# A weight's load moved behind the turn of u, and two x chunks loaded between the z writes, in a Fourier-filter and FFN kernel

## The chip, the cores and the metric

The kernel runs on one core of a Trainium2 chip. The metric is the device time in microseconds (us) of one execution. Every run of a kernel is paired with runs of the kernel before on the same chip.

## The reference

```python
X = np.fft.rfft(x, axis=1)                    # x: 8 batches, 3008 rows, 256 columns
Y = X * (filt_r + 1j * filt_i)[None, :, :]
y = np.fft.irfft(Y, n=3008, axis=1)           # 24064 rows in all
h = np.maximum(y.reshape(24064, 256) @ w_in, 0.0)   # w_in 256 x 2048
out = (h * h) @ w_out                               # w_out 2048 x 256, float32
```

The kernel does the transform in matmul stages (a: x to u, b: u to products with the filter, P: products to z, y: z to y). u and z go through DRAM to be turned. The FFN is a row of numbered steps: each computes two blocks of h for a group of 512 rows (psH), and half of an output tile of the group before (psO). The transforms of batches 1 to 7 are spread over those steps by a plan; batch 0's transform is the prologue, ahead of the first FFN step.

## The kernel before

These are the parts that the change touches, cut. Tiles of one pool and one tag take turns in the same bytes: `p_h2` has two buffers for the tag `h2`.

```python
def load_win():
    w32s[0] = p_h2.tile([128, 2, DFF], F32, tag="h2", name="win32")     # fp32 copy
    nc.sync.dma_start(out=w32s[0], in_=moe_w_in.rearrange(...))
def cast_win():                                # four GpSimd casts to fp16
    for k in range(4):
        nc.gpsimd.tensor_copy(out=sWin[...], in_=w32s[0][...])
def cast_wout(k):                              # one of four VectorE casts
    nc.vector.tensor_copy(out=sWout[...], in_=w32s[1][...])
...
uT = p_h2.tile([128, 2, NC, 128], F16, tag="h2", name="uT")   # batch 0's u, to be turned
...                                            # casts of x, constants
load_win()
cast_win()
for c in (0, 2, 1, 3):
    chunk_a0(c)                                # matmuls of stage a, copies to uT
for k in range(6):
    turn_u(k)
...                                            # 14 rounds of stages b and P:
    if r == 7:
        load_x(1, 0); cast_x(1, 0, nc.gpsimd)  # first x chunk of batch 1
    if r == 10:
        read_z(0, 0, (0,))
...
chunk_a(1, 0)                                  # stage a of that chunk
load_wout()
load_x(1, 1); load_x(1, 2)
... read_z(0, c) ...
write_u(1, 0)
keep_warm(14)                                  # unused matmuls on zeros
for n in range(4):
    unit_y(0, n)                               # first y; then the FFN steps start
```

## Time and profile before

| kernel before | |
|---|---|
| median of its runs beside the changed kernel | 848.89 us (848.24 to 850.38, 4 runs) |
| profiled run | 849.39 us, span 847.3 us, mean granted clock 0.977 |
| TensorE busy | 787.1 us, 93% |

The page cuts the span into 40 slices of 21.2 us. The digit is the busy share of TensorE (PE), or its granted clock, in tenths.

```profile
span 847.3 us, 14755 instructions
...
PE   3297888789999999999999999999999999999998
...
PEclk7599999999999999999999999999999999999999
```

The time is in the 9s, and they are full; only the first ten digits leave room. The prediction reads that room. Timeline columns: start, duration, engine, line, operation, and in brackets the idle time before it and what ended it.

```profile
73.70 1.02 PE L346 MATMUL psA<-x,sC 94*96 94x512 f16 x4 [2.09 <-POOL x L313]
...
75.28 4.81 PE L250 MATMUL warm<-zero 128*128 128x512 f16 x14 [0.56 <-DVE u L356]
...
79.93 0.27 PE L483 MATMUL psY<-zero 128*128 128x256 f16 x1
...
87.70 0.69 DVE L305 CAST sWout<-wout 128x1024 f16<-128x1024 f32 x1 [0.34 <-DMA wout<-in_moe_w_out_dram]
...
94.71 0.38 PE L327 MATMUL psA<-x,sC 94*96 94x512 f16 x1 [1.52 <-DVE x L313]
```

They are stage a of batch 1's first x chunk ahead of the FFN, the unused matmuls that are meant to keep the clock up (`keep_warm`), the first y, the first cast of W_out, and the first stage-a matmul inside the FFN steps.

### The profile page before, as it was taken

The page shows a single profiled execution, that of the slowest core. Times are in us where ns is not written, and L with a number is a line of the kernel's source. Part 1 is how long each engine was busy: PE and PEld are TensorE (multiplying, and loading weights), DVE is VectorE, ACT ScalarE, POOL GpSimd, SP SyncE. Part 2 cuts the span into 40 slices and gives each one's busy share as a digit, 9 for nine tenths or more (in the row PEclk, how much of TensorE's full clock was granted, in tenths as well). Part 3 has the DMA queues.
Part 4 walks back from the last instruction along what each step waited for, and adds up shares of the span by engine and source line. Part 5 has one row for each costly group of instructions (what it writes and reads, how often), then busy time and mean ns, then how long its engine had stood idle before and what let it go on. Part 6 is the DMA issues. An engine that isn't in the chain of part 4 may idle for free.

```text
span 847.3 us, 14755 instructions
## 1 busy us (share of the span) xinstructions
PE 787.1 (93%) x6084; PEld 554.0 (65%) x6084; DVE 548.7 (65%) x876; ACT 553.6 (65%) x709; POOL 30.8 (4%) x44
## 2 busy tenths in 40 slices
PE   3297888789999999999999999999999999999998
PEld 1273555566677766676677766686676767676666
DVE  3174856655896569955896569955896569753332
ACT  0174755567677767777677767777776767766663
POOL 4200013200000000000000000000000000000000
PEclk7599999999999999999999999999999999999999
DMA  9308844443467255633556255633466252341111
GB/s 365 160 13 235 203 135 137 125 113 100 142 163 169 65 160 138 180 82 100 160 146 171 62 161 137 181 82 100 148 155 168 62 164 63 90 98 38 38 38 51
DMA packets 87930, 107.94 MB, mean 127 GB/s; under 512 B 6208, under 2 KB 78656, under 8 KB 83392
## 3 DMA queue, kind: packets, MB, share of 16 engines
q1 hardware_dynamic: 87512, 106.59, 44.7%
q8 instruction: 47, 0.77, 0.4%
q10 hardware_dynamic: 288, 0.43, 0.2%
q14 instruction: 19, 0.16, 0.1%
q0 software_dynamic: 64, 0.00, 0.0%
HBM read 58.76 MB, written 48.23 MB: 126 GB/s over the span
## 4 chain that ended last, share of the span: by engine, by line
PE 79%; DMA 11%; DVE 5%; POOL 2%; ACT 1%; issue 1%; SPq 1%; POOLq 0%; DVEq 0%; ACTq 0%
PE psO L530 35%; PE psH L515 33%; PE psA L327 3%; DMA ut<-dU 3%; PE psY L485 2%; PE psB L408 2%; DVE prod L411 2%; PE psP L444 2%; DMA win<-in_moe_w_in_dram 2%; DMA f<-in_filt_r_dram 2%; DMA x<-in_x_dram 2%; DMA zt<-dZ 1%; DMA dZ<-ze 1%; DVE h L523 1%; POOL yf L420 1%; POOL yf L419 1%
## 5 line engine op out<-in xcount | busy, mean ns | idle before, releaser
L519 ACT ACTIVATE h<-psH 128x1024 f16<-128x1024 f32 x376 | 385.1, 1025 | 196.9 <-PE psH L515 196.9
L530 PE MATMUL psO<-sWout,h 128*128 128x256 f16 x3008 | 389.4, 273 | 2.6 <-DVE h L523 2.6
L515 PE MATMUL psH<-yt,sWin 128*128 128x512 f16 (+7 forms) x1728 | 387.9, 352 | 2.6 <-DVE yt L494 1.9
L530 PEld LDWEIGHTS <-h 128*128 128x128 f16 x3008 | 290.8, 98 | 82.4 <-DVE h L523 2.8
L523 DVE TENSOR_TENSOR h<-h 128x1024 f16<-128x1024 f16 x376 | 254.1, 685 | 100.8 <-ACT h L519 99.5
L515 PEld LDWEIGHTS <-sWin 128*128 128x128 f16 x1728 | 159.7, 98 | 103.3 <-issue 4.9
L411 DVE TENSOR_TENSOR prod<-psB,sF 128x1024 f16<-128x1024 f32 x96 | 116.7, 1220 | 11.4 <-PE psB L408 8.2
L494 DVE CAST yt<-psY 128x376 f16<-128x376 f32 x64 | 35.1, 549 | 64.5 <-PE psY L485 64.5
L446 ACT CAST ze<-psP 128x512 f16<-128x512 f32 x96 | 56.0, 586 | 31.1 <-PE psP L444 27.6
L334 DVE CAST u<-psA 96x512 f16<-96x512 f32 x54 | 37.1, 686 | 48.4 <-PE psA L327 48.4
L537 ACT COPY ost<-psO 128x512 f32<-128x512 f32 x94 | 55.4, 589 | 7.5 <-PE psO L530 5.8
L426 DVE TENSOR_TENSOR yf<-prod,yf 128x512 f16<-128x512 f16 x84 | 35.7, 425 | 19.4 <-POOL yf L420 17.0
L485 PEld LDWEIGHTS <-zt 112*128 112x128 f16 x512 | 34.8, 98 | 15.1 <-issue 5.1
L485 PE MATMUL psY<-sC,zt 112*128 112x94 f16 x512 | 42.1, 205 | 2.5 <-DMA zt<-dZ 2.5
L327 PE MATMUL psA<-x,sC 94*96 94x512 f16 x108 | 41.2, 381 | 1.5 <-DVE x L313 1.5
L408 PE MATMUL psB<-ut,sSB 128*128 128x256 f16 x192 | 36.6, 272 | 5.1 <-DMA ut<-dU 2.6
L444 PE MATMUL psP<-yf,sSP 128*128 128x256 f16 x168 | 32.4, 275 | 6.5 <-DVE prod L411 4.4
L408 PEld LDWEIGHTS <-sSB 128*128 128x128 f16 x192 | 18.7, 98 | 26.8 <-issue 7.5
L492 ACT CAST yt<-psY 128x376 f16<-128x376 f32 x64 | 29.8, 467 | 6.3 <-PE psY L485 6.2
L313 DVE CAST x<-x 94x2048 f16<-94x2048 f32 x27 | 32.8, 1217 | 0.0
L369 PE MATMUL psA<-sC,x 128*128 128x96 f16 x64 | 8.8, 246 | 25.5 <-ACT uT L377 25.3
L332 ACT CAST u<-psA 96x512 f16<-96x512 f32 x54 | 30.9, 572 | 0.9 <-DMA x<-in_x_dram 0.9
(53 smaller groups left out, 239.8 us busy)
## 6 DMA issues: line engine op xcount, KB each, us to landing
x<-in_x_dram SPq DMA_DIRECT2D x24, 768.0 KB
dZ<-ze SPq DMA_DIRECT2D x32, 384.0 KB
zt<-dZ SPq DMA_DIRECT2D x64, 192.0 KB
dU<-u SPq DMA_DIRECT2D x28, 384.0 KB
out_dram<-ost SPq DMA_DIRECT2D x32, 256.0 KB
out_dram<-ost SPq DMA_DIRECT2D x64, 128.0 KB
ut<-dU SPq DMA_DIRECT2D x7, 1024.0 KB
ut<-dU SPq DMA_DIRECT2D x7, 512.0 KB
```

The costliest lines, as they stand in the source:

```text
L327: nc.tensor.matmul(ps[0:96, :], sSA, x16s[(b, c)][:, 2 * i:2 * i + 2, :], start=True, stop=True)
L334: nc.vector.tensor_copy(out=o, in_=pv)
L408: nc.tensor.matmul(ps[:, i * D:(i + 1) * D], sSB[:, 2 * p + i, :], uts[b][:, 2 * p + i, :], start=True, stop=True)
L411: nc.vector.tensor_mul(out=prod, in0=ps.rearrange("p (a d) -> p a d", d=D).unsqueeze(1).to_broadcast([128, 2, 2, D]), in1=sF[:, :, 2 * p:2 ...
L444: nc.tensor.matmul(ps[:, i * D:(i + 1) * D], sSP[:, c2, :], prod[:, i, :], start=True, stop=True)
L446: nc.scalar.copy(out=zes[(b, c)][:, 2 * i6:2 * i6 + 2, :], in_=ps.rearrange("p (a d) -> p a d", d=D))
L485: nc.tensor.matmul(ps[:, 94 * jj:94 * jj + 94], zt[:, 4 * (g % 2) + jj, dt * 128:(dt + 1) * 128], sSY, start=True, stop=True)
L515: nc.tensor.matmul(ps[:, i, o:o + n], sWin[:, dt, jt * 128:(jt + 1) * 128], yts[b][:, dt, r:r + n], start=(dt == 0), stop=(dt == 1))
L519: nc.scalar.activation(out=h2[:, 2 * s:2 * s + 2, :], in_=ps, func=AF.Relu)
L523: nc.vector.tensor_mul(out=v, in0=v, in1=v)
L530: nc.tensor.matmul(pso[g][:, t % 2, :], h2s[g][:, jt, t * 128:(t + 1) * 128], sWout[:, jt, :], start=(jt == 0), stop=(jt == NJT - 1))
L537: nc.scalar.copy(out=ost, in_=pso[g])
```

## The change

uT takes the bytes that hold the fp32 copy of W_in until that is cast. The intent of the first part is to turn the order round: u is turned first, and W_in takes over the buffer. The second part loads two chunks of batch 1's x in the prologue instead of one, and moves batch 1's plan ahead by up to two steps.

```diff
-    load_win()
-    cast_win()
-
     for c in (0, 2, 1, 3):
         chunk_a0(c)
...
         turn_u(k)
+    load_win()
+    cast_win()
...
-        if r == 7:
-            load_x(1, 0)
-            cast_x(1, 0, nc.gpsimd)
+        if r in (5, 8):
+            load_x(1, r // 8)
+            cast_x(1, r // 8, nc.gpsimd)
...
-    chunk_a(1, 0)
+    for c in range(2):
+        chunk_a(1, c)
     load_wout()
-    load_x(1, 1)
     load_x(1, 2)
+    load_x(1, 3)
...
-    write_u(1, 0)
-    keep_warm(14)
+    for c in range(2):
+        write_u(1, c)
+    keep_warm(10)
... and in the plan of batch 1:
-            for c in range(1, 4):
-                put(5 + 2 * c, 0, cast_x, 1, c)
-            put(7, 0, load_x, 1, 3)
-        t0 = 6
-        for a in range(4 if b == 1 else 0, 16):
+            for c in range(2, 4):
+                put(3 + 2 * c, 0, cast_x, 1, c)
+        t0 = 4 if b == 1 else 6
+        for a in range(8 if b == 1 else 0, 16):
...
-        put(14, 1, read_u, b)
-        t0 = 17 if b == 1 else 18
+        put(12 if b == 1 else 14, 1, read_u, b)
+        t0 = 16 if b == 1 else 18
...
-            r = t0 + (16 if b == 1 else 19) * p // 11
+            r = t0 + (17 if b == 1 else 19) * p // 11
```

## The prediction

> **What bounds the kernel now.** I read the windows view first, cut where the kind of work changes, to see where TensorE (the PE column) is not full. Columns: window, length, busy time and count of each engine, granted clock, DMA share, GB/s.
>
> ```profile
> 0.00:34.00 34.00, 6.86 (x22) 2.65 (x23) 6.63 (x11) 1.28 (x1) 13.98 (x19) 0.65 0.82 327
> 34.00:80.00 46.00, 37.12 (x367) 29.17 (x367) 25.98 (x28) 24.62 (x36) 2.11 (x2) 0.89 0.29 78
> 80.00:95.00 15.00, 11.11 (x75) 5.50 (x74) 10.48 (x17) 10.31 (x13) 0.00 (x0) 1.00 1.05 266
> 95.00:115.00 20.00, 19.31 (x140) 12.62 (x138) 13.05 (x20) 13.38 (x19) 0.00 (x0) 1.00 0.63 180
> 115.00:165.00 50.00, 39.73 (x273) 26.45 (x274) 32.54 (x46) 26.76 (x35) 14.69 (x24) 0.97 0.45 128
> 300.00:830.00 530.00, 527.91 (x4047) 373.96 (x4045) 365.35 (x602) 375.93 (x474) 0.00 (x0) 1.00 0.43 116
> ```
>
> From 300 to 830 TensorE is busy 527.9 of 530: nothing there is touched by the change and nothing there can be won. What can be won is ahead of 180 us: 27 us of TensorE idle before 34, and 10 us between 115 and 165. So the second view is the timeline of the start, and the third that of VectorE (DVE) after 115.
>
> ```profile
> 10.42 0.26 PE L371 MATMUL psA<-sC,x 120*128 120x96 f16 x1 [2.69 <-DVE x L611]
> 12.18 2.02 POOL L611 CAST x<-x 128x1024 f16<-128x1024 f32 x2 [9.51 <-DMA x<-in_x_dram]
> 15.82 0.39 SPq L293 DMA_DIRECT2D win<-in_moe_w_in_dram  x1
> ...
> 30.22 4.00 POOL L301 CAST sWin<-win 128x1024 f16<-128x1024 f32 x4 [7.97 <-DMA win<-in_moe_w_in_dram]
> 30.25 1.28 ACT L377 ACT_TABLE_LOAD   x1 [30.25 <-DMA win<-in_moe_w_in_dram]
> 34.25 0.48 ACT L377 CAST uT<-psA 128x384 f16<-128x384 f32 x1 [2.72 <-POOL sWin L301]
> 34.78 0.24 PE L369 MATMUL psA<-sC,x 128*128 128x96 f16 x1 [23.63 <-ACT uT L377]
> ```
>
> TensorE starts batch 0's first transform at 10.42 and stops after a few matmuls for 23.6 us. It waits for ScalarE to copy the first result into uT. ScalarE waits for the last W_in cast. uT has the same bytes as the fp32 copy of W_in, so W_in must arrive (30.2) and be cast (34.2) before uT may be written. A weight that nobody reads before 81.8 us holds up everything.
>
> ```profile
> 115.06 0.39 PE L408 MATMUL psB<-ut,sSB 128*128 128x256 f16 x2 [0.49 <-DMA ut<-dU]
> ```
>
> ```profile
> 115.49 1.23 DVE L411 TENSOR_TENSOR prod<-psB,sF 128x1024 f16<-128x1024 f32 x1 [1.04 <-PE psB L408]
> 118.16 0.43 DVE L426 TENSOR_TENSOR yf<-prod,yf 128x512 f16<-128x512 f16 x1 [1.45 <-POOL yf L420]
> 118.50 0.69 DVE L523 TENSOR_TENSOR h<-h 128x1024 f16<-128x1024 f16 x1
> 119.11 1.22 DVE L411 TENSOR_TENSOR prod<-psB,sF 128x1024 f16<-128x1024 f32 x1
> 121.69 0.43 DVE L426 TENSOR_TENSOR yf<-prod,yf 128x512 f16<-128x512 f16 x1 [1.36 <-POOL yf L420]
> ```
>
> From 115 to 164 the second batch's twelve products run on VectorE, each followed by a 1.4 us wait for two GpSimd copies; the squares of the FFN queue behind. VectorE has no other idle time there: it sets the pace.
>
> **What the Trainium skill says.** "TensorE: Matmul & The Clock Gate", Part 1, says an idle TensorE falls to half clock and needs a free-running window of about 3.4 us of activity to come back. The trace agrees: after the long idle the 96-column matmuls start 0.08 us apart until 40.5, and 0.045 apart from 41.35. "SBUF — State Buffer", "SBUF: two separate sides", says that GpSimd and VectorE exclude each other on a shared port only where VectorE uses both its ports or has two SBUF inputs. The new GpSimd cast will lie beside products that read one operand from PSUM, so by that page it should not block; no run yet shows it. "DMA: Bandwidth & Descriptors", "Issuing engines are not separate DMA queues", says all DMAs share sixteen engines and interleave. The 80 to 95 window, with a DMA share of 1.05, agrees: W_out, issued at 76.35, was first used at 87.70, 11.3 us for 2 MB, while W_in alone moved at about 430 GB/s.
>
> **The change, part by part.**
>
> *1. W_in behind the turn of u.* uT's first write no longer waits for W_in. The list of waits of the built kernel shows what is left: the same bytes held the third x piece, so the first copy waits for its load (landed 12.18) and its two GpSimd casts (done 14.2). The ScalarE table load needs only the load and hides under the casts. The first copy thus moves from 34.25 to 14.2: 20.0 us. It does not gain the full 23.6 us of the idle. Work behind it must be ready 20 us earlier: the filter casts end at 22.3 and are first used at 49.06 - 20.0 = 29.0; the DFT constants had landed when W_in began to move, about 24.5, and are used at 34.8. Both fit. W_in itself is now issued when the turn's last matmul is done (48.2 - 20.0 = 28.2), needs about 5 us for its 2.1 MB plus about 2, and 4.0 for the casts: ready near 39.5, against a first use near 61.8. Hidden. The clock recovers at about the same distance from the start of work, give or take 1 us. So the whole prologue moves by 20.0.
>
> *2. Two x chunks between the z writes.* The second chunk takes, in time, the place of the one there was: issued behind the second z write, landing some 6 us later, cast in 1.9. In before the first matmul on it began at 73.70, 2.1 us after the last unit; now the first chunk's four matmuls (1.0 us) fit into that hole, and the second starts near 53.7. No cost, and no gain here either: y waits for the z write (72.26, 3.15 us) and the reads behind it, which move by 20.0 only. Four fewer warming matmuls save nothing if y waits for z; at best 1 us, which step 4 eats.
>
> *3. The FFN steps behind.* Four psA matmuls leave the steps. Before: from the first psA (94.71) to the first psB (115.06) 20.35 us: six steps with two psA each, 13.05 us or 2.175 each, two steps with y, then a step in which psB waits for ut. After: four steps at 2.175 (8.70), two bare ones at 1.74 (3.48; the distance of bare steps near 170 us), and the y steps with the following psH, 107.76 to 112.50 (4.74): 16.92 us. The first psB comes 3.43 us earlier. Its data is there: the last copy of u ended 13.1 us after the first psA and ut landed 7.2 later; now 8.7 + 7.2 = 15.9, 1 us in hand. The VectorE chain then has the same 12 products, GpSimd waits and sums, the same two x and two y casts, but by the listing of both builds 17 squares in place of 16: +0.60. Both kernels issue the last product in step 33, so what follows is alike. Net 2.8.
>
> *4. Contention, given back.* W_out and two x chunks share the engines as before, but the second x issues about 2 us earlier and one more u write of 0.4 MB follows (its wait list holds it until W_out has landed). VectorE waited only 0.3 us for W_out and was then packed until 94.6, so a late W_out or a late x counts in full. An estimate: 0.39 MB at the 266 GB/s of that window is 1.5 us, of which I take 0.6.
>
> Sum: 848.4 - 20.0 - 2.8 + 0.6 = 826.2 us; I predict 826.
>
> **Rivals.**
> *A, the wait changes its name.* Constants, filter casts or the x piece replace W_in, and the prologue gains only 15 or so. For it: the DMA engines are full from 3 to 29 us. Against it: the landing times above leave 5 us or more for each. It would give about 831.
> *B, W_out's loading becomes the floor.* FFN steps 3 to 7 need W_out, issued only behind the z reads. If x takes bandwidth from it, 2 to 3 us of the gain go. For it: DMA share 1.05 in 80 to 95 and VectorE packed behind it. Against it: W_out's issue moves by the same 20 us. It would give about 828.
> *C, the gain is swallowed later.* If VectorE's chain in the second batch were tied to something absolute, earlier arrival would become waiting. Against it: the trace shows it waiting only for GpSimd and its own order, all of which move. It would give 840 or more; I give it almost nothing.
> *D, more than the sum.* If the clock comes up a window sooner, or y starts earlier because warming ends sooner, 1 to 3 us more: 823 to 825.
>
> **Range and chances.** The 20.0 is read off two recorded times and is good to 1 us; the 2.8 rests on two chains and is good to 1.5; the contention may be 0 to 2.5. Together 822.5 to 829.5 should hold it 8 times in 10. Two per cent is 17 us, a limit of 831.4; even with all of step 3 lost and 2 us of contention the first step alone gives 830. Faster 0.95, same 0.04, slower 0.01.
>
> **What would show it right or wrong.** Step 1: ScalarE's first uT copy at 14.2 behind a GpSimd x cast, no idle of 20 us on TensorE, W_in cast near 35 to 40. Wrong if that copy starts later, or TensorE waits for a filter cast or a constant. Step 2: the second chunk's matmuls near 53.7, y near 60. Step 3: from first psA to first psB about 17 us, from the first product to the last sum of batch 1 about 49 us. Step 4: first W_out cast near 67.7 to 68.5; later means rival B. From 180 us on both traces must match, shifted; a stretch there with TensorE idle would prove me wrong.

## More of the kernel before

The three batches of experiments ran on three different chips, so kernels of different batches are compared only through their ratios to the kernel before.

## The result, and the profile after

The changed kernel takes 824.38 us (median of 4 runs: 826.93, 823.8, 822.26, 824.96), against 848.89 before. The ratio is 0.971, with a 95% interval from 0.9678 to 0.9742. A ratio is the mean time of one kernel's runs over that of the other's of the same rounds, so it is not quite the ratio of the medians. The outputs are correct.

The profile is of the 826.93 us run, the slowest of the four. The same three lines of its page:

```profile
span 824.8 us, 14748 instructions
...
PE   5878987999999999999999999999999999999998
...
PEclk7998999999999999999999999999999999999999
```

The 3 and the 2 at the start have become 5 and 8. The windows view of the changed kernel (length, then busy time and count of TensorE, weight loads, VectorE, ScalarE and GpSimd; granted clock, DMA share, GB/s) shows where it still has room:

```profile
0.00:34.00 34.00, 21.32 (x230) 16.39 (x231) 17.09 (x25) 9.86 (x15) 10.18 (x15) 0.85 0.81 313
34.00:60.00 26.00, 22.02 (x175) 15.88 (x174) 16.84 (x16) 17.33 (x25) 7.77 (x6) 0.93 0.68 187
60.00:75.00 15.00, 10.59 (x59) 4.68 (x57) 9.61 (x16) 9.33 (x13) 0.00 (x0) 0.92 1.05 267
75.00:92.00 17.00, 16.54 (x107) 10.55 (x107) 9.77 (x15) 9.89 (x14) 0.00 (x0) 0.87 0.47 125
92.00:142.00 50.00, 41.11 (x294) 27.00 (x292) 33.00 (x47) 29.00 (x38) 13.40 (x22) 0.99 0.43 125
...
280.00:806.00 526.00, 524.65 (x4027) 371.97 (x4025) 363.73 (x600) 373.16 (x470) 0.00 (x0) 1.00 0.42 116
```

In the first 34 us TensorE is busy 21.3 us instead of 6.9. The late part is as full as it was. What is new lies between 60 and 92: DMA share 1.05, TensorE idle for 4.4 us, then a granted clock of 0.87. The timeline of the changed kernel gives the events:

```profile
12.02 1.28 ACT L377 ACT_TABLE_LOAD   x1 [12.02 <-DMA x<-in_x_dram]
14.03 0.48 ACT L377 CAST uT<-psA 128x384 f16<-128x384 f32 x1 [0.73 <-POOL x L610]
...
28.31 0.39 SPq L293 DMA_DIRECT2D win<-in_moe_w_in_dram  x1
...
37.18 3.99 POOL L301 CAST sWin<-win 128x1024 f16<-128x1024 f32 x4 [15.15 <-DMA win<-in_moe_w_in_dram]
...
54.37 1.02 PE L346 MATMUL psA<-x,sC 94*96 94x512 f16 x4 [1.89 <-POOL x L313]
55.23 4.01 PE L250 MATMUL warm<-zero 128*128 128x512 f16 x10
...
56.11 0.42 SPq L297 DMA_DIRECT2D wout<-in_moe_w_out_dram  x1
...
59.08 0.27 PE L483 MATMUL psY<-zero 128*128 128x256 f16 x1
...
68.46 0.69 DVE L305 CAST sWout<-wout 128x1024 f16<-128x1024 f32 x1 [1.89 <-DMA wout<-in_moe_w_out_dram]
...
75.47 0.59 PE L327 MATMUL psA<-x,sC 94*96 94x512 f16 x1 [0.89 <-DVE x L313]
75.84 1.91 PE L530 MATMUL psO<-sWout,h 128*128 128x256 f16 x8
...
94.24 0.38 PE L408 MATMUL psB<-ut,sSB 128*128 128x256 f16 x2
```

ScalarE's first copy to uT has moved from 34.25 to 14.03, and it now waits for a GpSimd cast of x instead of the W_in casts. W_in is ready at 41.2, long before the first FFN step. The first y moves by 20.85 us. In both kernels it starts right behind the last unused matmul, with no idle time between (no bracket on its line): TensorE does not wait for z there. VectorE then waits 1.89 us for W_out (0.34 before), and some time behind that a group of eight psO matmuls takes 1.91 us where it usually takes 1.04: TensorE is at half clock. The windows view in stretches of 3.4 us, laid so that one starts where the half clock does, shows what came ahead of it:

```profile
65.50:68.90 3.40, 3.37 (x25) 1.77 (x24) 1.13 (x2) 3.40 (x5) 0.00 (x0) 1.00 1.05 236
68.90:72.30 3.40, 1.64 (x11) 0.65 (x9) 3.40 (x7) 2.22 (x4) 0.00 (x0) 1.00 1.00 214
72.30:75.70 3.40, 1.67 (x4) 0.55 (x4) 3.40 (x6) 1.24 (x2) 0.00 (x0) 0.52 1.01 216
75.70:79.10 3.40, 3.40 (x13) 1.88 (x12) 1.19 (x3) 0.58 (x1) 0.00 (x0) 0.50 0.63 190
```

VectorE has no idle time from 68.9 to 75.7 (3.40 of 3.40, twice): it works off what the late W_out held up. TensorE waits for it and is busy 1.64 of 3.40 us. In the next stretch its clock is halved, and stays so for a further one until it has been busy throughout. So the late weight goes with two costs in this profile: 1.9 us of wait, and half clock behind it.

The starts of the same events, from the timelines of six profiled runs (the last four are experiments below; "rest" is from the last sum of batch 1's filter products to the end of the span):

| start of, us | before | changed | warm_steps | warm_both | before_both | wout_pool |
|---|---|---|---|---|---|---|
| first copy of u | 34.25 | 14.03 | 14.21 | 14.15 | 34.25 | 11.24 |
| first y matmul | 79.93 | 59.08 | 59.40 | 59.02 | 78.54 | 58.88 |
| first W_out cast (VectorE) | 87.70 | 68.46 | 66.81 | 69.91 | 85.89 | - |
| first psA in the steps | 94.71 | 75.47 | 74.86 | 76.91 | 93.94 | 72.03 |
| first psB of batch 1 | 115.06 | 94.24 | 91.78 | 93.83 | 114.24 | 88.94 |
| last sum of batch 1 | 163.66 | 143.36 | 140.96 | 142.94 | 163.41 | 138.12 |
| rest | 683.6 | 681.4 | 678.8 | 681.0 | 679.8 | 681.8 |
| span | 847.3 | 824.8 | 819.8 | 823.9 | 843.2 | 819.9 |

Before against changed, stage by stage: to the first y -20.85, to the first W_out cast +1.61, to psA 0.00 (7.01 us in both), to psB -1.58, to the last sum +0.52, rest -2.2. Together -22.5 us of span, for this slowest run of the changed kernel.

### The profile page after: what moved, and what is told of

It reads as the page before. It is cut to its first block, busy times and chain, and to the rows that moved or that the text cites.

```text
span 824.8 us, 14748 instructions
## 1 busy us (share of the span) xinstructions
PE 787.3 (95%) x6080; PEld 553.7 (67%) x6080; DVE 547.7 (66%) x874; ACT 553.4 (67%) x708; POOL 32.6 (4%) x45
## 4 chain that ended last, share of the span: by engine, by line
PE 83%; DMA 8%; DVE 6%; POOL 2%; ACT 1%; issue 1%; SPq 0%; POOLq 0%; DVEq 0%; ACTq 0%
PE psO L530 36%; PE psH L515 34%; PE psA L327 3%; PE psY L485 2%; DMA ut<-dU 2%; PE psB L408 2%; DVE prod L411 2%; PE psP L444 2%; DMA wout<-in_moe_w_out_dram 1%; DVE h L523 1%; DMA x<-in_x_dram 1%; DMA dZ<-ze 1%; DMA zt<-dZ 1%; POOL yf L420 1%; POOL yf L419 1%
## 5 line engine op out<-in xcount | busy, mean ns | idle before, releaser
L426 DVE TENSOR_TENSOR yf<-prod,yf 128x512 f16<-128x512 f16 x84 | 35.7, 425 | 19.4 <-POOL yf L420 16.9
L419 DVE COPY yf<-prod 64x512 f16<-64x512 f16 x72 | 20.9, 290 | 2.5
```

## The experiments

Twelve kernels ran, four to a batch: a_again, p1_only, p2_only and own_early on one chip (median of the kernel before there: 849.45 us), warm_steps, x3_late, late_plan and wout_pool on a second (848.14), the last four on a third (848.22). All gave correct outputs, and all were timed in five rounds.

### The change again, and its two parts alone

The first is the changed kernel with no edit. The other two are the kernel before with one part of the diff above.

```diff
# p1_only: load_win() and cast_win() behind turn_u, nothing else
# p2_only: the two x chunks and the new plan; load_win() and cast_win() stay ahead of chunk_a0
```

> The changed kernel once more, unaltered, for a second profile and more times. In its first profile TensorE ran at half clock from 72.7 to 79.3 us, because it had idled while VectorE waited for W_out; I put the cost at 1.9 us (18.77 us instead of 16.92 from the first psA matmul to the first psB). If that drop depends on where the clock's window happens to fall, the second profile may lack it and then shows about 17 us there. If it belongs to the schedule, the profile shows 18.5 to 19 us again. Time: 822 to 827 us, median near 824.5.

> Only the first half of the change: W_in is loaded and cast behind the turn of u, everything else as before. My theory (shared bytes held the start back by 20.0 us, the rest of the schedule only moves): first uT copy near 14.1 us, total 848.9 - 20.0 = 829 us (828 to 830.5). Rival C (later stages swallow part of it): 833 or more. If this half alone gives 824 to 825, then the second half is worth nothing.

> Only the second half: two x chunks of batch 1 between the z writes and the shifted plan of batch 1, with W_in loaded early as before. My theory: the step from the first psA matmul to the first psB is about 17 us instead of 20.35, the chain on VectorE about 0.5 us longer, and W_out some 1 us later: 846 to 847 us. If it alone gives 843 to 844, the whole surplus over 20 us comes from it; if it is 848 to 849, the plan is worth nothing and the surplus comes from elsewhere.

Measured: a_again 826.78 us (822.92 to 827.75, 5 runs), ratio 0.9724 [0.9697, 0.975]. p1_only 829.31 (827.59 to 833.97, 6 runs), 0.9771 [0.9743, 0.9798]. p2_only 844.32 (842.1 to 847.97, 6 runs), 0.9946 [0.992, 0.9972].

By means, p1_only gains 19.7 us, p2_only 5.0, and both together 23.9: the parts add up within the intervals. The first is the 20.0 of the prediction. In p1_only's trace the first copy of u starts at 14.28. The first y, at 61.40, moves by only 18.5 us there: the cast of x ahead of it moved by 19.4, and TensorE was at half clock for the four matmuls on that chunk (1.86 us, 1.02 before). The second part gained more than the 2.2 us that I had left of it (2.8 less 0.6); its interval, 2.4 to 6.8 us, holds the 2.8 but not the 2.2. The 846 to 847 us expected of p2_only were missed. Its six times, too, have a gap (842.1 to 842.96, and 845.67 to 847.97), and its profile, of the slowest, shows what the changed kernel's does: 1.81 us of wait for W_out, then half clock and 19.09 us from psA to psB.

The changed kernel's nine times so far lie, by eye, in two groups, 822.3 to 825.0 and 826.8 to 827.8. a_again's profile, from the upper group, again shows a wait for W_out (2.23 us) and half clock from 73 to 80 (18.71 us from psA to psB). That raised the question of the next batches: what separates the groups?

### W_in early, but uT in other bytes

```diff
-    uT = p_h2.tile([128, 2, NC, 128], F16, tag="h2", name="uT")
+    uT = sF[:, 1].rearrange("p c d -> p (c d)").rearrange("p (t c q) -> p t c q", t=2, c=NC)
```

This is the kernel before in its order. Only the bytes of uT differ: a part of sF that is not yet in use.

> The kernel before with its order kept (W_in loaded and cast early), but uT put in bytes that nobody else uses at that time, those of the half of sF that is written after the turn. It separates the shared bytes from the early load itself. My theory, that only the sharing cost time: the first uT copy comes when the first matmuls are done, near 11.1 us, 23 us earlier than before, and the total is about 826 us (824.5 to 827.5), although W_in still arrives near 30 us. Rival (the early W_in load itself delays the start through the DMA engines): the first copy stays later than 14 us and the total is above 829 us.

Measured: 826.78 us (825.83 to 828.77, 4 runs), ratio 0.974 [0.9717, 0.9763]. ScalarE in its timeline:

```profile
1.61 1.28 ACT L377 ACT_TABLE_LOAD   x1 [1.61 <-PEq L700]
11.20 0.48 ACT L377 CAST sF<-psA 128x384 f16<-128x384 f32 x1 [8.30 <-PE psA L371]
```

The copy waits for its matmul and for nothing else, although W_in still goes first and is cast only from 31.38. So it was the shared bytes that held up u, not W_in's place in the queue. This gains 22.4 us by means without moving a load.

### Unused matmuls in FFN steps 3 to 7

```diff
             ffn_g1(g, k)
+            if g == 0 and k >= 3:
+                keep_warm(3)
```

This is the changed kernel with three matmuls on zeros in each of those steps, so that TensorE does not fall to half clock while VectorE works off W_out.

> The changed kernel with three dummy matmuls on zeros (0.2 us each) after the first product of each of the FFN steps 3 to 7, where TensorE otherwise idles for W_out's casts. Two profiles of the changed kernel had half clock there and its nine times fall in two groups, 822 to 825 and 826.8 to 827.8. My theory (whether the clock falls depends on where its window lies, and costs about 1.8 us): the profile shows the full clock from 62 to 92 us, about 17 us from the first psA to the first psB matmul instead of 18.7, and times of 821 to 825 us, with the upper group thinned. Rival (the spread comes from the DMA engines or from elsewhere): the times stay at 822 to 828 with a median above 825, or get longer.

Measured: 822.82 us (820.85 to 822.91, 5 runs), ratio 0.9691 [0.9668, 0.9714].

```profile
66.81 0.69 DVE L305 CAST sWout<-wout 128x1024 f16<-128x1024 f32 x1
...
74.86 0.38 PE L327 MATMUL psA<-x,sC 94*96 94x512 f16 x1 [0.60 <-DVE x L313]
...
91.78 0.38 PE L408 MATMUL psB<-ut,sSB 128*128 128x256 f16 x2
```

From psA to psB it is 16.92 us, the prediction's number, and the clock is full from 62 to 92. The missing 1.85 us of the changed kernel's 18.77 was half clock. But W_out also came without a wait in this profile, which no unused matmul explains. I took the absence of the upper group for the clock's doing; warm_both below shows that this was too quick.

### The last x chunk's load later

```diff
     load_x(1, 2)
-    load_x(1, 3)
... in the plan of batch 1:
+            put(3, 1, load_x, 1, 3)
```

> The changed kernel with the load of the fourth x chunk of batch 1 moved from the prologue to FFN step 3, behind W_out. It tests the term for contention. My theory (W_out was slowed by the second x load issued beside it): W_out reaches VectorE in about 11.3 us after its issue instead of 12.3 and 12.8, VectorE waits for it 1 us less, and the time falls by 0.5 to 1.5 us against the changed kernel. Rival (W_out is slow because of the z reads and the total bytes, not this load): W_out still takes over 12 us, same time.

Measured: 824.04 us (822.32 to 826.52, 5 runs), ratio 0.9711 [0.9687, 0.9735]: no gain on the changed kernel's 0.971 and 0.9724. The theory was that this load slows W_out. The timeline says no:

```profile
55.38 0.42 SPq L297 DMA_DIRECT2D wout<-in_moe_w_out_dram  x1
...
68.48 0.69 DVE L305 CAST sWout<-wout 128x1024 f16<-128x1024 f32 x1 [1.47 <-DMA wout<-in_moe_w_out_dram]
```

From the issue of W_out to its first cast it is 13.1 us with that load out of the way. With it in place, profiles show 12.35 (changed), 14.02 (a_again), 11.1 (late_plan) and at most 10.6 (warm_steps). So W_out can be late without this load. One profile among times that differ so much does not exclude that the load has some share. The added u write is out as a cause: in the changed kernel's trace SyncE waits 5.1 us for W_out to land before it issues that write.

### The two chunks, but the plan as before

```diff
-        t0 = 4 if b == 1 else 6
+        t0 = 6
-        put(12 if b == 1 else 14, 1, read_u, b)
-        t0 = 16 if b == 1 else 18
+        put(14, 1, read_u, b)
+        t0 = 17 if b == 1 else 18
-            r = t0 + (17 if b == 1 else 19) * p // 11
+            r = t0 + (16 if b == 1 else 19) * p // 11
```

> The changed kernel with its two early x chunks, but the plan of batch 1 as before (psA from step 10, ut read in step 14, first psB in step 17). It splits the 2.8 us of the third part: by my working the four psA matmuls that left the steps are worth 0.9 us, and starting the VectorE chain a step earlier, with no wait for ut, the other 1.9. So this should be about 1.9 us slower than the changed kernel (mean of nine runs 825.1): 826 to 828.5. If the shifted plan is worth nothing, it is 825.

Measured: 824.36 us (823.38 to 825.58, 4 runs), ratio 0.9715 [0.9691, 0.9739]. That is no slower than the changed kernel; the expectation of 826 to 828.5 failed.

```profile
72.73 1.04 PE L530 MATMUL psO<-sWout,h 128*128 128x256 f16 x8
...
76.20 0.38 PE L327 MATMUL psA<-x,sC 94*96 94x512 f16 x1
```

In the changed kernel step 8 begins with a psA, which waits for VectorE's cast of x; its first psO starts only behind that. Here psO of step 8 starts at once, and psA follows two steps later. The step that the earlier plan saves is largely spent waiting for x, and one square fewer then lies in the VectorE chain (48.6 us from psB to the last sum, instead of 49.1).

### W_out out of the FFN's way

```diff
-    uT = p_h2.tile([128, 2, NC, 128], F16, tag="h2", name="uT")
+    uT = sF[:, 1].rearrange("p c d -> p (c d)").rearrange("p (t c q) -> p t c q", t=2, c=NC)
...
+    load_win()
+    cast_win()
+    load_wout()
+    for k in range(4):
+        cast_wout(k)          # now on GpSimd instead of VectorE
     for c in (0, 2, 1, 3):
         chunk_a0(c)
... load_win, cast_win, load_wout and the four cast_wout of the plan gone from their places
```

> A version that should beat both. uT lies in the idle half of sF (first copy near 11.2 instead of 14.0), W_in is loaded early as in the kernel before, W_out behind it into the same buffer as soon as W_in is cast, and W_out is cast on GpSimd, idle there, instead of VectorE. By my theory this takes 2.8 us off the start, the wait for W_out (1.9 to 2.2 us) and most of the 2.4 us of W_out casts off VectorE, and TensorE no longer idles long enough there to lose its clock (1.8): 817 us (815 to 820). Rival: W_out's load beside the first z writes delays z and y, and half of it is lost: 821 or more.

Measured: 820.13 us (818.88 to 821.67, 4 runs), ratio 0.9666 [0.9642, 0.9689]. It beats both kernels: by 28.3 us the kernel before, and by some 4 us the changed one, if the ratios are compared (0.9666 and 0.971). W_out is cast from 43.76 on GpSimd, the first psA comes at 72.03, and no W_out wait is left. It is 3 us short of what I expected: the first y comes at 58.88, as in the changed kernel, although the first copy of u is 2.8 us earlier (11.24). The second x cast starts at 52.24 (52.43 in the changed kernel), and the matmuls on that chunk, ten unused ones and y follow it; so the gain at the start is lost ahead of that cast. Also the clock is half again from 50.75 to 57.75 and from 136 to 139.5.

### Unused matmuls in two places, in four kernels

The last batch adds two more unused matmuls per step where half clock was seen near 140 us.

```diff
         ps = psH(f"psH_{g}_{s}")
+        if 24 <= 8 * g + s <= 33:
+            for _ in range(2):
+                nc.tensor.matmul(ps[:, 0, :], zero[:, 0:128], zero, start=True, stop=True)
... and keep_warm(3) in steps 3 to 7 as in warm_steps
# warm_both: on the changed kernel.   late_both: on late_plan.   before_both: on the kernel before.
# best2: on wout_pool, with W_out's casts moved behind the two x casts on GpSimd
```

> The changed kernel with three unused matmuls on zeros behind the first product of FFN steps 3 to 7 (as in warm_steps) and two more in front of the second products of steps 24 to 33, where half clock was seen near 140 us. The clock theory: no stretch of half clock after 60 us, from the first psA to the first psB 16.9 us as in warm_steps, time 821 to 822.5 and a spread of its runs under 1.5 us. The rival, that the spread comes from DMA timing: still two groups some 3 us apart, and no gain on warm_steps' 822.8.

> The same unused matmuls in late_plan (two x chunks ahead of the FFN, but batch 1's plan of steps as before). My prediction gave the earlier plan 1.9 of its 2.8 us: then 1.5 to 2.5 us slower than warm_both. The revised view, that the earlier plan only makes its first psA wait for the x cast: within 0.7 us of warm_both.

> The kernel before with the same unused matmuls. If half clock in these two places cost it nothing much (its window near 161 us, and none between 80 and 100), it takes 846.5 to 848 us, 0.5 to 2 less than before, and the difference to warm_both, free of the clock, is 25 to 26 us against the 22.8 predicted without contention. If the clock cost both kernels the same, the difference stays at 24.3.

> wout_pool (uT in other bytes, W_in early, W_out behind it and cast on GpSimd) with W_out's casts moved behind the x casts on GpSimd, and the same unused matmuls. If wout_pool's missing 3 us lay in x casts queued behind W_out's casts and in late half clock: 816 to 818 us. If they lay in W_out's transfer beside the z writes: no better than 819.5.

Measured:

| run | median us (range, runs) | ratio to before [95%] |
|---|---|---|
| warm_both | 824.82 (822.32 to 826.71, 6) | 0.9721 [0.9696, 0.9745] |
| late_both | 825.99 (823.81 to 826.21, 5) | 0.9728 [0.9704, 0.9752] |
| before_both | 845.86 (844.47 to 848.08, 6) | 0.9972 [0.9948, 0.9995] |
| best2 | 823.25 (821.55 to 824.45, 6) | 0.9705 [0.9682, 0.9729] |

*warm_both* missed. Its six times are 822.32, 823.38, 823.66 and 825.98, 826.04, 826.71: two groups some 3 us apart, as the rival said, and no gain. Yet the clock is full from 58 to 153 us in its profile, which is of the upper group (half clock, which the expectation had ruled out, comes once more from 153.4 to 156.8, behind the added matmuls):

```profile
69.91 0.69 DVE L305 CAST sWout<-wout 128x1024 f16<-128x1024 f32 x1 [3.40 <-DMA wout<-in_moe_w_out_dram]
...
93.83 0.38 PE L408 MATMUL psB<-ut,sSB 128*128 128x256 f16 x2
```

W_out came 13.94 us after its issue, and VectorE waited 3.40. From psA to psB it is again 16.92. So half clock in the two places with added matmuls is not needed for a time of the upper group. The arrival of W_out fits better, though not alone: of the 4.1 us between the spans of warm_steps and warm_both the stretch from the first y to the first psA, with W_out in it, has 2.4, and the rest behind batch 1's last sum has 2.2. The profiles in the upper group waited for it 1.89 (changed), 2.23 (a_again), 1.47 (x3_late) and 3.40 us (warm_both); those in the lower group 0 (warm_steps) and 0.60 (late_plan). p2_only's wait of 1.81 in its own upper group fits too. late_both's profile (826.06) is an exception: no wait for W_out, but half clock from 105 to 112. Only one run of each kernel has a profile, so this is a match over eight profiles with one exception, not a proof.

*late_both* is 0.6 us above warm_both by means (825.31 against 824.68), within the 0.7 of the revised view, though the intervals (some 2 us each way) do not exclude 1.5. Nor do the profiles compare the plans cleanly: warm_both's waited 3.40 us for W_out and late_both's not at all.

*before_both* gained 2.6 us by means, somewhat more than expected, and its distance to warm_both is 21.3 us, where I expected 25 to 26. The table of starts shows why: its W_out came without a wait (first cast at 85.89), warm_both's with 3.40 us of it. Between these two profiles the first y moves by -19.52, W_out takes back 3.54, of which 1.05 returns by the first psA, and psA to psB gives -3.38 against the predicted -3.43. Against warm_steps, in whose profile W_out is also in time, before_both's stages move by -19.14 to the first y, +0.06, 0.00 and -3.38, near the prediction's -20.0 and -3.43 with no contention. (These two ran on different chips, and warm_steps lacks the later unused matmuls.)

*best2* missed, and on its chip gained less than wout_pool on its own. The windows views of wout_pool, then of best2, while the FFN starts:

```profile
64.00:72.00 8.00, 6.96 (x43) 3.32 (x42) 6.48 (x11) 7.56 (x10) 0.00 (x0) 1.00 0.86 214
```

```profile
64.00:72.00 8.00, 8.00 (x51) 3.91 (x50) 4.76 (x8) 6.50 (x8) 0.00 (x0) 1.00 0.93 206
```

With W_out no longer in the way, TensorE is nearly the bound there. In best2 it is busy 8.00 of 8.00: the unused matmuls, fifteen of some 0.21 us, are no longer in idle time. From the first y to psA it takes 14.86 us instead of 13.15. The y start is no earlier either (59.21). The remedy for a wait has probably become a cost once the wait was gone; best2 also moved the W_out casts, so the two are not separated. Half clock does not recur between 60 and 180 us in its profile, and its span is no shorter for it. Neither of the two theories of the expectation had this in it. The kernel that best2's order makes without the unused matmuls was not run.

## Why the prediction was right, point by point

The time, 826.0 predicted and 824.38 measured, lies in the range; faster was the right class.

*Step 1 was right, in mechanism and in size.* The first copy of u came at 14.03 for 14.2, behind the GpSimd cast of x that was named, and p1_only alone gave 19.7 us for 20.0. Rival A is out: no constant or filter cast took W_in's place. The only miss is W_in's landing: the casts ran from 37.18 to 41.2, ready near 39.5 in the prediction. It stayed hidden. own_early adds that the shared bytes were the whole of it.

*Step 2 was right on the second chunk, and wrong on what holds y.* The chunk's matmuls began at 54.37 for 53.7, and y at 59.08 for 60. But the step let y wait for z, so that fewer unused matmuls would save nothing, and no trace shows that wait: in all fourteen profiles the first y starts without idle time behind the last unused matmul. The unused matmuls held TensorE for 4.65 us before (fourteen, 75.28 to 79.93) and for 3.85 us now (ten, 55.23 to 59.08). These 0.8 us are nearly all that y gained beyond 20.0. In the profiled run they were of no use, because VectorE then waited for W_out, which was issued 20.24 us earlier (76.35, now 56.11). How many could go before y waits for z was not tested. The first GpSimd cast of x took 1.89 us (48.06 to 49.95) beside VectorE products that read PSUM, as it did in the kernel before (71.75), where VectorE was idle beside it. That is what the Trainium skill's page "SBUF — State Buffer", section "SBUF: two separate sides", led the prediction to expect; the trace agrees.

*Step 3 was right in structure, and its term "16.92" holds only at full clock.* Two runs with the clock kept up gave 16.92 exactly, but the changed kernel's own two profiles show 18.77 and 18.71. The prediction had the half clock only in the prologue. Its VectorE term was +0.60, and +0.52 came. What the step credited to the earlier plan is in doubt: late_plan and late_both, with the old plan, came within about 1 us of their partners.

*Step 4 was right in place, wrong in cause, and too small.* The first W_out cast came at 68.46, inside the 67.7 to 68.5 that were given, but neither the second x load nor the added u write is needed for it: W_out was late without the one (x3_late), and the other is issued only when W_out has landed. W_out's own time from issue to first cast went from at most 10.5 to 14.0 us between executions of kernels alike in that place. Its wait, 0 to 3.4 us, with 1.8 to 2.2 us of half clock behind it in four profiles (psA to psB of 18.71 to 19.09 us for 16.92), stands where the sum had 0.6. Rival B had the place and about the size; its reason, that x takes bandwidth, is not shown, and it is a cost of some runs and not of all. W_in, loaded with nothing else moving, took from 7.3 to 9.1 us between issue and cast in eight profiles, so other loads of this kernel are not needed for a spread. The windows view shows where W_in's comes from. In all eight nearly all of the 2.1 MB moves within 7 us of the issue. In five nothing comes much later, and the cast starts 7.3 to 7.6 us after the issue. In the other three (changed, x3_late, warm_both) the DMA engines move one or two more pieces alone (82 GB/s for 0.1 us each, so some 8 KB), 0.5 to 1.3 us behind the rest, and the cast starts after 8.8 to 9.1. Whether W_out is late for the same reason cannot be seen beside its neighbours: its cause stays open.

*The end was near the prediction partly because misses cancelled.* In the profiled run the first W_out cast moved by 19.24 us, where steps 1 and 4 together have 19.4: the issue moved by 20.24, and from there to the cast it took 1.00 us longer, where step 4 has 0.6. Behind it 1.85 us of half clock, which no step had, were met by 2.2 us less in the rest, which no step had either. That the sum came so near is in part luck. That rest varies from 678.8 to 683.6 us between the profiles in the table, and half clock lies in or just ahead of it in several. In the profiles the trace was not "matched, shifted" to better than some 2 us, as the prediction had asked. Rival C is not needed. Of rival D, y starting earlier because the warming ends sooner is what the traces show, with 0.8 us. By means the second part gained 4 to 5 us for 2.2; the intervals are too wide to say whether that needs a cause of its own.

## What to carry to other kernels

When an early write waits for a late-needed load, look at the bytes before the order: tiles that share a buffer wait for each other, and another place for one of them can be worth as much as a reordering. When a long wait is taken away, the next limit can be a transfer that used to land just in time, as W_out here; ask how many tenths of a microsecond of slack it has, and by how much its duration varies between runs. Unused matmuls hold up the clock at no cost only while TensorE would be idle; measure them again after every change that removes the idle time. And look at what an instruction waits for in the trace before you reason on it: y stood behind unused matmuls, not behind its data.

## What the Trainium skill lacked or had wrong

- "TensorE: Matmul & The Clock Gate", Part 1, gives, in its table of states, "≥1 idle window" of about 3.4 us as what leads to half clock; further down it has a kernel in which short idle stretches were enough, without a share. The runs agree on the length (stretches of some 3.4 and 7 us) but not on idleness: the 3.4 us ahead of half clock had TensorE busy for 1.64 us (changed kernel, 68.90 to 72.30) and 1.34 us (137.30 to 140.70, and wout_pool before 136.00). A window that is more than half idle was enough here.
- The same part puts the ramp penalty below 1% of a typical span and advises not to fit a count of slow matmuls. The size agrees (1.85 us of 825 in psA to psB), but here it is as large as other terms of the prediction, so it had to be counted.
- "DMA: Bandwidth & Descriptors", section "Issuing engines are not separate DMA queues", says that transfers interleave; neither it nor the rest of that page has a figure for the spread of one transfer between executions. Here W_out took from at most 10.5 to 14.0 us and W_in 7.3 to 9.1 us from issue to first cast, with the same transfers around them or fewer.
- I found no page that tells of tiles which share a buffer in turns and the wait that this makes. It was worth 20 us here (34.25 to 14.03 for the first copy of u).
